# Two tiled groups per batch, with T and the slot reads in the h banks of PSUM

## The chip, the cores and the metric

The kernel runs on one core of a Trainium2 chip. The metric is the device time of one execution in microseconds (us). The engines named below are TensorE (PE, matmuls; PEld is its weight load), VectorE (DVE), ScalarE (ACT), GpSimd (POOL) and SyncE (SP, which only starts transfers here). PSUM, the memory that matmuls write to, has eight banks of 512 fp32 values per partition, as the kernel's pools divide it.

## The reference

An attention block is followed by a feed-forward block. For each of 8 batches and 8 heads there are 512 tokens `x` and 32 slots `state`, each of width 64:

```python
scores = scale * np.matmul(x, state.transpose(0, 1, 3, 2))
a = softmax(scores)                      # over the 32 slots
xread = np.matmul(a, state)              # 512 rows per head
scores2 = scale * np.matmul(state, x.transpose(0, 1, 3, 2))
a2 = softmax(scores2)                    # over the 512 tokens
sread = np.matmul(a2, x)                 # 32 rows per head: the slot reads
y = concatenate([xread, sread], axis=2)  # heads side by side: 4352 rows of 512
h = y @ w_in                             # 512 -> 2048
g = s * relu(h) ** 2 + b
out = g @ w_out                          # 2048 -> 512
```

(`softmax` stands here for the reference's max, exp and division.)

## The kernel before, in words

**The products.** The same scores serve both softmaxes. For a batch b, `T_mm` multiplies the state by the transposed tokens: T holds the scores of all 8 heads, in two PSUM banks (one per half of the tokens), 16 small matmuls of 64x32 weights with 256 columns. `E_exp` on ACT takes four exponentials of it (E, with row sums that serve the second softmax). `D_mm` sums E over the slots of each head, `D_ln` and `D_exp` make the reciprocal R of that sum, and `a4_mul` multiplies E by R: a is the first softmax, transposed. The token reads are never made. Instead `M_mm` multiplies the state by w_in (M, four chunks c of 512 columns; each chunk is 8 small matmuls into two banks), `M_cast` copies each bank into SBUF (one on DVE, one on ACT, or as the planner likes), and `h_mm` computes h = a x M, 16 blocks f of 128 columns, two matmuls each. `relu` on ACT reads a block of h, `square` on DVE squares two blocks at once. The scalars `s` and `b` are applied to the output.

The second product, o, is made for batch 0 in the plain way (`rows_mm`) and for batches 1 to 7 by a scheme of seven products of half matrices in place of eight (`STEPS`, `step_mm`), which needs sums of g blocks (`pair_sums`: pd, on DVE) and of w_out blocks (`weight_sum`: u). Two banks hold o, and DVE empties them (`step_out`), after which POOL or SP sends the rows out.

The slot reads of a batch are V (`V_mm`: E transposed by the tokens, 32 small matmuls of 64 columns). E is transposed by a DMA on SP's queue (`aT_dma`), the result is scaled by `V_copy` on DVE and transposed once more by a DMA (`sr_dma`). All eight batches' slot reads are multiplied at the very end, as h_sr and osr.

**Tiled mode.** T, M, V and one sum for the bias use parts of the TensorE array (`tp=` gives the part): several such small matmuls run beside one another. Everything else uses the whole array. The name "tiled group" is used below for tiled matmuls that follow one another with nothing else between.

**PSUM.** Eight banks: pool `psA` (planner's name "att") has four, for T of batches 2 to 7, D, M, V and small things; `psH` ("h") has two, for h; `psO` has two, for o. T of batches 0 and 1 uses the o banks, which are free then.

**The order.** Nothing is ordered by hand. Every piece of work is given to a planner by `add` with its engine and estimated duration, a priority key (lower goes first), what it needs and makes, and the buffers it uses. `Plan.order` plays the work through on its own clock, and the kernel then issues the instructions of every engine in the order found. On the chip each engine follows its order strictly and waits by semaphore where something isn't ready. The table K holds the numbers that keys are made of. For the work around the change (lines 654 to 749): T of batch b has key `kT`, the four M chunks have `kM[0..3]`, and V has `kV`, each an operation of its own; the planner adds 0.1 to the duration when the tiled mode changes, and prefers tiled work while it is in tiled mode. Lines 128 to 131 model a load: `channel` is the time when the DMA channel is free.

**The loads.** `SEQ` (line 374) is the order in which POOL starts the loads of w_in (wi0 to wi3), w_out (wo0 to wo3) and tokens of batches 0 to 3 in fp16 (x0 to x3). The fp16 tokens of batches 0 and 1 are read only by V; those of later batches are also transposed by DMA for T (`dma_xT`). Batches 0 and 1 have their tokens transposed on TensorE instead (`xT_mm`) from an fp32 load at the start. `filler` is a matmul on zeros [...].

Of the kernel before, what the change touches and what calls it, by code (L numbers as in the profile page):

```python
# [13 lines left out]
class Plan:  # L14
# [13 lines left out]
    def order(self, filler, fill_until, ready):  # L28
# [46 lines left out]
        while done_n < len(ops) and now < getattr(self, "horizon", 1e9):  # L75
            for e in free_at:
                if free_at[e] > now + 1e-9:
                    continue
                best = None
                alone = False  # L80
                if e == "PE" and not mode:
                    near = [i for i in cand[e] if ops[i][7] and since[i] <= now + 0.3 and soon(i) <= now + 0.3]
                    alone = len(near) < 2 or sum(len([b for b in ops[i][5] if self.pool_of[b] == "att"]) for i in near[:2]) > (
                        self.caps["att"] - sum(x not in freed for x in allocs["att"])
                    )
                look = self.look if e in ("ACT", "DVE") else 0.06
                for i in cand[e]:
                    if since[i] > now + look:
                        continue
                    t = soon(i) - now  # L90
                    if t > look:
                        continue
                    k = ops[i][1] + 20.0 * max(0.0, t)
                    if e == "PE" and ops[i][7] and mode:
                        k -= 4.0
                    if alone and ops[i][7]:
                        k += self.solo if now < 40.0 else self.late
                    if len(ops[i][0]) > 1 and e == "DVE":
                        k += ops[i][9]
                        if free_at["ACT"] <= now + 0.3:  # L100
                            continue
                    if best is None or k < best[0]:
                        best = (k, i, t)
                if best is not None and best[2] > 1e-9:
                    continue
                if best is None:
                    fill = 0.22
                    if e == "PE" and now < fill_until and not allocs["h"] and not any(since[i] < now + fill for i in cand[e]):
                        free_at[e] = now + fill
                        times.append(free_at[e])  # L110
                        log.append((now, len(log), "PE", filler, "warm", free_at[e]))
                    continue
                i = best[1]
                engs, key, fn, needs, makes, bufs, land, tiled, after, spare = ops[i]
                for x in engs:
                    cand[x].discard(i)
                for b in bufs:
                    if b not in placed:
                        placed.add(b)
                        allocs[self.pool_of[b]].append(b)  # L120
                dur = engs[e]
                if e == "PE":
                    dur += 0.1 * (tiled != mode)
                    mode = tiled
                end = done = now + dur
                if land is not None:
                    kind, span = land
                    if kind == "load":
                        done = max(channel, end + 2.0) + span
                        channel = max(channel, done)  # L130
                        done += 0.8
                    elif kind == "tp" and e == "SP" and now < channel + 4.0:
                        done = end + max(span, min(8.0, 6.0 - 0.75 * (now - channel)))
                        channel = max(channel, now + 2.0) + 1.1
                    else:
                        done = end + span
                free_at[e] = end
                times.append(end)
                times.append(done + self.hop)
                for m in makes:  # L140
                    ready[m], made_on[m] = done, (e if land is None else None)
                for m in makes:
                    for j in waits.pop(m, ()):
                        count[j] -= 1
                        if count[j] == 0:
                            settle(j)
                for b in bufs:
                    users[b] -= 1
                    if users[b] == 0:
                        freed[b] = done + self.hop  # L150
                done_n += 1
                log.append((now, len(log), e, fn, makes, end))
# [9 lines left out]
def kernel(  # L162
# [21 lines left out]
    P = 128  # L184
# [25 lines left out]
    def att_ps(shape, dtype, name):  # L210
        return psA.tile(shape, dtype, tag="att", name=name)
# [45 lines left out]
    for i in range(4):  # L257
# [15 lines left out]
    ident32 = konst.tile([P, P], FP32, name="ident32")  # L273

    K = dict(
        h1=18.7, hs=1.0, M0=-6.0, M1=3.8, T1=10.0, x2=31.5, T2=21.6, D2=25.6, M2=44.7, V0=39.2, V1=31.3, u=25.2,
        us=-12.3, pd1=16.9, o0=20.4, o2=33.9, w=24.1, r=5.8, T=-9.2, D=7.2, Mb=4.3, V=9.4, S=2.5, S0=-1.1,
        E=-2.4, L=-5.7, E0=-4.8, L0=10.2, E1=-17.5, L1=-2.0, a4=-9.1, Mc=13.9, pd=19.2, solo=18.7, f0=6.6,
        f1=17.4, mc=-12.6, hsr=-6.4, Ssr=-3.2, jE00=18.1, jE01=15.1, jL00=3.9, jL01=20.6, jR00=5.7, jR01=-5.2,
        jE10=5.7, jE11=-10.7, jL10=-6.2, jL11=-11.3, jR10=0.8, jR11=-2.5, jM0=-2.7, jM1=2.1, xc=3.9, a2=31.2,  # L280
        lx=10.0, la=5.4, lb=12.1, rs=33.5, xs=10.6, x1=10.8, rL=6.4, a4L=-9.7, McL=4.7, mcL=2.1, soloL=3.3,
    )
    A = {b: {"E": {}, "a4": {}} for b in range(B)}
    G, PD, U, SN, OSB = {}, {}, {}, {}, {}
# [40 lines left out]
    def PEt(t):  # L325
        return ("PE", t)
# [44 lines left out]

    gate = konst.tile([P, 2], FP16, name="gate")
    nc.gpsimd.tensor_copy(gate, xf_part(0, 2)[:, 0, 0:2])
    SEQ = "wi0 wi1 wi2 wo0 wo1 wi3 wo2 x2 wo3 x0 x1 x3"
    seq = [(t[:-1], int(t[-1])) for t in SEQ.split()]
    for n, it in enumerate(seq):
        key = -40 + n
# [107 lines left out]
    def xT_copy(b, p):  # L485
# [5 lines left out]

        return fn

    def st_T(b, g, q, m):
        h = head_of(g, q)
        if b < 4:
            return A[b // 2]["stT"][64 * m : 64 * m + 64, 8 * (b % 2) + h]
        return stTd[64 * m : 64 * m + 64, (b - 4) * NG + h // 4, 32 * (h % 4) : 32 * (h % 4) + 32]

    def T_mm(b, gs):  # L500
        def fn(e):
            a = A[b]
            if gs[0] == 0:
                if b < 2:
                    a["T"] = [ob[m].rearrange("p (g t) -> p g t", g=NG) for m in range(2)]
                else:
                    a["T"] = [att_ps([P, NG, S // 2], FP32, f"T_{b}_{m}") for m in range(2)]
            for q in range(4):
                for g in gs:
                    h = head_of(g, q)  # L510
# [100 lines left out]

    def V_mm(b):
        def fn(e):
            ps = A[b]["V"] = att_ps([P, NG, D], FP32, f"V_{b}")
            for g in range(NG):
                for c in range(SCH):
                    for q in range(4):
# [36 lines left out]
    for b in range(B):  # L654
# [5 lines left out]
            kM = [8 * c + (K["M0"] if b == 0 else K["M1"]) for c in range(4)]  # L660
        elif b == 2:
            kx, kT, kD = K["x2"], K["T2"], K["D2"]
            kM = [K["M2"] + i for i in range(4)]
        else:
            kT = NKF * b + K["T"]
            kx, kD = kT - 12, kT + K["D"]
# [9 lines left out]
        if b < NB_T:  # L676
            for p in range(4):
                ps = ("att", f"xTps{b}{p}")
                kp = kx + K["xs"] * p
                add(  # L680
                    PEt(0.55), kp, xT_mm(b, p), [("xf", b, p), "ident32"] + ([("xTps", b, p - 1)] if p else []),
                    [("xTps", b, p)], [ps, ("u", f"xf{2 * b + p // 2}"), xT_b],
                )
                add(
# [8 lines left out]
                )  # L693
        xT_need = [("xTh", b, p // 2, p % 2) for p in range(4)] if b < NB_T else [("xT4", b, i) for i in range(4)]
        E_b = [("E0", f"E{b}0"), ("E1", f"E{b}1"), ("rs", f"rs{b}")]
        Tb = [("att", f"T{b}0"), ("att", f"T{b}1")] if b >= 2 else []
        if b == 0:
            for g in range(2):
                add(
                    PEt(0.2), kT, T_mm(b, [g]), [("stT", b), ("xTh", b, g, 0), ("xTh", b, g, 1)] + ([("T", b, 0)] if g else []),  # L700
                    [("T", b, g)], Tb + [xT_b] + stT_b + E_b, tiled=True,
                )
        else:
            add(
                PEt(0.22), kT, T_mm(b, [0, 1]), [("stT", b)] + xT_need + ([("E", 0, 0), ("E", 0, 1)] if b == 1 else []),
                [("T", b, 0), ("T", b, 1)], Tb + [xT_b] + stT_b + E_b, tiled=True,
            )
        for g in range(2):
            Eb, Rb, a4b = (f"E{g}", f"E{b}{g}"), (f"R{g}", f"R{b}{g}"), (f"a4{g}", f"a4{b}{g}")
# [16 lines left out]
                add(AC(0.63), K["rs"] + 2 * b + g, E_sum(b, g), [("E", b, g)], [("sum", b, g)], [Eb, rs], after=24.0)  # L726
        q_need = [("sum", b, 0), ("sum", b, 1)] if b < 2 else [("E", b, 0), ("E", b, 1)]
        add(DV(0.25), kD + 4, q_rec(b), q_need, [("q", b)], [rs, ("q", f"q{b}")])
        M_b = ("M", f"M{b}")
        for c in range(4):  # L730
            mp = [("att", f"M{b}{c}{g}") for g in range(2)]
            add(
                PEt(0.22), kM[c], M_mm(b, c), [("stT", b), ("wi", c)], [("Mps", b, c)], mp + stT_b + [M_b],
                tiled=True,
            )
            for g in range(2):
                kc = kM[c] + K["Mc" if b < 2 else "McL"] + K.get(f"jM{b}", 0.0)
                add(
                    (AC(0.53), DV(0.6)) if g else (DV(0.6), AC(0.53)), kc, M_cast(b, c, g),
                    [("Mps", b, c)], [("M", b, c, g)], [mp[g], M_b], spare=K["mc" if b < 2 else "mcL"],  # L740
                )
        kV = [K["V0"], K["V1"]][b] if b < 2 else NKF * b + K["V"]
        V_b = ("att", f"V{b}")
        add(
            PEt(0.22), kV, V_mm(b), [("aT", b, 0), ("aT", b, 1)] + ([("x", b, i) for i in range(4)] if b < 2 else []), [("V", b)],
            [V_b, ("aT", f"aT{b}"), xn_b], tiled=True,
        )
        add(DV(0.25), kV, V_copy(b), [("V", b), ("q", b)], [("sr", b)], [V_b, ("sr", f"sr{b}"), ("q", f"q{b}")])
        add(("SP", 1.2), kV, sr_dma(b), [("sr", b)], [("srT", b)], [("sr", f"sr{b}")], ("tp", 4.0))


# [401 lines left out]
```

The softmax here doesn't subtract the row's maximum and nothing guards it: scores larger than these inputs give would overflow.

## Time and profile before

| what | value |
|---|---|
| median of 4 runs | 210.35 us (209.77 to 211.1) |
| the profiled execution: its own time | 209.84 us |
| the profiled execution: span of the trace | 208.0 us |
| DVE g squares (L791), 64 | 43.5 us, 685 ns each |
| ACT ReLU of h (L784), 127 | 73.4 us, 600 ns each |
| M casts on ACT (L305), 37 | 20.6 us, 602 ns each |
| M casts on DVE (L307), 27 | 17.8 us, 685 ns each |
| matmuls of Mps, 256 | started from 12.7 to 151.4 us |
| matmuls of T in att banks, 96 | started from 51.3 to 147.8 us |
| matmuls of V, 256 | started from 43.8 to 172.9 us |

The page gives busy time of each engine and, in the slices, its share in each of 40 equal parts of the span. A row of a group has the line, the engine, what is written from what, the count, and the mean duration. The duration of a matmul includes its passage through the array, so matmuls that follow one another overlap in the rows; how long one occupies TensorE is read from the distance between starts.

### The profile page before, as it was taken

How to read it: one execution, taken by the hardware profiler on the slowest of the kernel's cores; microseconds unless marked ns; L12 is line 12 of the kernel's file. 1: busy time of each engine (PE TensorE's matmuls, PEld its weight loads, DVE VectorE, ACT ScalarE, POOL GpSimd, SP SyncE). 2: the span in 40 equal slices, each digit the busy share in tenths (PEclk: the TensorE clock that was granted, in tenths of full speed). 3: DMA queues.
4: the chain of work that ended last, by engine and by line, in shares of the span. 5: the costliest groups of instructions: out<-in, count | busy, mean ns of one | idle time of the engine just before them, and what ended most of it. 6: DMA issues, size and time to landing. Idle time of an engine off the chain costs nothing.

```text
span 208.0 us, 4904 instructions
## 1 busy us (share of the span) xinstructions
PE 202.6 (97%) x1957; PEld 133.2 (64%) x1957; DVE 168.1 (81%) x334; ACT 133.1 (64%) x297; POOL 42.8 (21%) x67
## 2 busy tenths in 40 slices
PE   7998999999999999999999999999999999999993
PEld 3743444343866775577667775777657777888882
DVE  3589988988768997989999997898789969686552
ACT  2579999875688468985398548954886545354000
POOL 0861000241160244011521134021102110110000
PEclk9999999999999999999999999999999999999999
DMA  6999999999999346961496338721212110311033
GB/s 193 306 204 195 205 209 190 175 245 144 187 168 159 110 126 126 138 102 50 103 138 126 106 76 140 146 101 52 81 31 101 48 58 6 104 40 62 4 125 126
DMA packets 44423, 26.05 MB, mean 125 GB/s; under 512 B 26480, under 2 KB 42608, under 8 KB 44400
## 3 DMA queue, kind: packets, MB, share of 16 engines
q0 software_dynamic: 14976, 15.73, 41.3%
q1 hardware_dynamic: 29136, 9.84, 24.5%
q8 instruction: 15, 0.25, 0.5%
q10 hardware_dynamic: 288, 0.16, 0.3%
q14 instruction: 8, 0.07, 0.1%
HBM read 19.43 MB, written 8.91 MB: 136 GB/s over the span
## 4 chain that ended last, share of the span: by engine, by line
PE 77%; DMA 16%; POOL 3%; DVE 1%; SPq 0%; issue 0%
PE o L214 44%; PE h L214 20%; DMA wo<-in_moe_w_out_dram 10%; DMA aT<-E 4%; PE h_sr L214 3%; PE osr L214 3%; PE Mps L214 3%; DMA xf<-in_x_dram 2%; POOL wi L342 1%; PE D L214 1%; PE V L214 1%; POOL wo L352 1%; PE T L214 1%; SPq L256 0%; POOL xn L365 0%; DVE c_sr L1040 0%
## 5 line engine op out<-in xcount | busy, mean ns | idle before, releaser
L784 ACT ACTIVATE g<-h 128x512 f16<-128x512 f32 x127 | 73.4, 600 | 28.4 <-PE h L214 27.1
L214 PE MATMUL h<-a,M 128*128 128x512 f16 x256 | 73.4, 379 | 0.6 <-ACT g L784 0.5
L214 PEld LDWEIGHTS <-pd 128*128 128x128 f16 x448 | 42.8, 98 | 19.9 <-issue 2.2
L214 PEld LDWEIGHTS <-g 128*128 128x128 f16 x400 | 38.7, 98 | 18.5 <-issue 1.4
L214 PE MATMUL o<-u,pd 128*128 128x256 f16 x336 | 49.8, 273 | 0.0
L791 DVE TENSOR_TENSOR g<-g 128x1024 f16<-128x1024 f16 x64 | 43.5, 685 | 4.7 <-ACT g L784 4.1
L214 PE MATMUL o<-wo,g 128*128 128x256 f16 (+1 forms) x288 | 45.3, 296 | 0.0
L1052 POOL DMA_DIRECT2D out_dram<-c x24 | 16.4, 682 | 105.1 <-DVE c L1040 96.9
L214 PEld LDWEIGHTS <-M 128*128 128x128 f16 x256 | 24.4, 98 | 12.8 <-issue 3.8
L1040 DVE SCALAR_TENSOR_TENSOR c<-o,sb_cols,bias_bc 128x512 f32<-128x512 f32 x28 | 21.0, 750 | 9.4 <-PE o L214 8.8
L305 ACT CAST M<-Mps 128x512 f16<-128x512 f32 x37 | 20.6, 602 | 8.1 <-PE Mps L214 8.0
L1040 DVE SCALAR_TENSOR_TENSOR c<-o,sb_cols,c 128x512 f32<-128x512 f32 x21 | 15.7, 749 | 6.8 <-PE o L214 6.6
L807 DVE TENSOR_TENSOR pd<-g 128x1024 f16<-128x1024 f16 x28 | 19.1, 683 | 0.1
L307 DVE CAST M<-Mps 128x512 f16<-128x512 f32 x27 | 17.8, 685 | 0.4
L214 PE MATMUL o<-u,g 128*128 128x256 f16 x112 | 16.6, 273 | 0.0
L365 POOL DMA_DIRECT2D xn<-in_x_dram x20 | 15.8, 828 | 3.9 <-DMA wi<-in_moe_w_in_dram 3.4
L214 PE MATMUL o<-wo,pd 128*128 128x256 f16 x112 | 15.1, 273 | 0.0
L816 DVE TENSOR_TENSOR pd<-g,pd 128x512 f16<-128x512 f16 x28 | 12.0, 430 | 0.3
L818 DVE TENSOR_TENSOR pd<-g,pd 128x512 f16<-128x512 f16 x28 | 11.8, 422 | 0.5
L529 ACT ACTIVATE E<-T 128x256 f16<-128x256 f32 x24 | 8.9, 384 | 5.1 <-PE T L214 5.0
L560 ACT ACTIVATE R<-L 128x512 f16<-128x512 f32 x16 | 10.1, 630 | 0.5
L553 ACT ACTIVATE L<-D 128x512 f32<-128x512 f32 x16 | 9.4, 595 | 1.2 <-PE D L214 1.0
(81 smaller groups left out, 160.6 us busy)
## 6 DMA issues: line engine op xcount, KB each, us to landing
out_dram<-c POOLq DMA_DIRECT2D x24, 256.0 KB, 2.5
xf<-in_x_dram SPq DMA_DIRECT2D x8, 256.0 KB, 4.8
wi<-in_moe_w_in_dram POOLq DMA_DIRECT2D x4, 512.0 KB, 8.5
wo<-in_moe_w_out_dram POOLq DMA_DIRECT2D x4, 512.0 KB, 16.1
xn<-in_x_dram POOLq DMA_DIRECT2D x4, 512.0 KB, 21.8
xn<-in_x_dram POOLq DMA_DIRECT2D x16, 128.0 KB, 4.4
out_dram<-osb POOLq DMA_DIRECT2D x4, 256.0 KB, 4.2
out_dram<-c SPq DMA_DIRECT2D x4, 256.0 KB, 2.5
```

Source lines behind the costliest of these rows:

```text
L214: return nc.tensor.matmul(out, lhsT, rhs, start=start, stop=stop, tile_position=tp, is_transpose=is_transpose, skip_group_check=True,)
L305: nc.scalar.copy(dst, src)
L307: ENG[e].tensor_copy(dst, src)
L365: nc.gpsimd.dma_start(out=xn[b][:, h0:h1].rearrange("p h c d -> p h (c d)"), in_=x[b, h0:h1].rearrange("h (q c) d -> q h (c d)", q=P),)
L560: nc.scalar.activation(A[b][f"R{g}"], A[b][f"L{g}"], AF.Exp, scale=-1.0)
L784: nc.scalar.activation(g_of(name, f), OSB["h", name, f], AF.Relu)
L791: ENG[e].tensor_mul(g, g, g)
L807: nc.vector.tensor_tensor(pd[:, :, 0:2], g4[:, :, 1:2, :].to_broadcast((P, 2, 2, t)), g4[:, :, 0:4:3, :], ALU.subtract,)
L816: nc.vector.tensor_tensor(pd[:, :, 2], g4[:, :, 3], pd[:, :, 0], ALU.subtract)
L818: nc.vector.tensor_tensor(pd[:, :, 3], g4[:, :, 2], pd[:, :, 2], ALU.subtract)
L1040: nc.vector.scalar_tensor_tensor(t, src, s_bc, add, ALU.mult, ALU.add)
L1052: ENG[e].dma_start(dst[:, rows:SCH:2, hD * h : hD * h + hD], SN[b, name])
```

## The change

In batches 2 to 7, T and the M chunks 0 and 1 are made one operation for the planner, with T's key, and the M chunks 2 and 3 and the slot reads of another batch a second one, with the key of chunk 2: batch 2 takes V of batch 0, batch 3 takes V of batches 1 and 2, and batches 4 to 7 take V of the batch before. V of batch 7 remains alone. For batches 0 and 1, T and the M chunks stay as they were. T of batches 2 to 7 and every V are written to banks of psH in place of psA. A helper `several` runs functions one after the other.

With it the planner's numbers change: nearly the whole table K, the modelled landing of a load before 15 us (0.1 behind the channel in place of 0.8), the duration of `xT_mm` (0.45 in place of 0.55), and x1 is loaded before x0.

```diff
-                        done += 0.8
+                        done += 0.8 if done > 15.0 else 0.1
...
-        h1=18.7, hs=1.0, M0=-6.0, M1=3.8, T1=10.0, x2=31.5, T2=21.6, D2=25.6, M2=44.7, V0=39.2, V1=31.3, u=25.2,
...
+        h1=16.1, hs=1.0, M0=-6.0, M1=4.5, T1=13.8, x2=17.3, T2=21.6, D2=23.7, M2=46.3, V0=38.1, V1=37.9, u=27.3,
...
-    SEQ = "wi0 wi1 wi2 wo0 wo1 wi3 wo2 x2 wo3 x0 x1 x3"
+    SEQ = "wi0 wi1 wi2 wo0 wo1 wi3 wo2 x2 wo3 x1 x0 x3"
...
+    def several(*fs):
+        def fn(e):
+            for f in fs:
+                f(e)
+
+        return fn
...
-                    a["T"] = [att_ps([P, NG, S // 2], FP32, f"T_{b}_{m}") for m in range(2)]
+                    a["T"] = [psH.tile([P, NG, S // 2], FP32, tag="h", name=f"T_{b}_{m}") for m in range(2)]
...
-            ps = A[b]["V"] = att_ps([P, NG, D], FP32, f"V_{b}")
+            ps = A[b]["V"] = psH.tile([P, NG, D], FP32, tag="h", name=f"V_{b}")
...
-            kM = [K["M2"] + i for i in range(4)]
+            kM = [K["M2"], K["M2"], K["M2"] + K["Mb"], K["M2"] + K["Mb"]]
...
-                    PEt(0.55), kp, xT_mm(b, p), [("xf", b, p), "ident32"] + ([("xTps", b, p - 1)] if p else []),
+                    PEt(0.45), kp, xT_mm(b, p), [("xf", b, p), "ident32"] + ([("xTps", b, p - 1)] if p else []),
...
-        Tb = [("att", f"T{b}0"), ("att", f"T{b}1")] if b >= 2 else []
+        Tb = [("h", f"T{b}0"), ("h", f"T{b}1")] if b >= 2 else []
...
+        if b >= 2:
+            vs = {2: [0], 3: [1, 2]}.get(b, [b - 1])
+            add(
+                PEt(0.66), kT, several(T_mm(b, [0, 1]), M_mm(b, 0), M_mm(b, 1)),
+                [("stT", b), ("wi", 0), ("wi", 1)] + xT_need,
+                [("T", b, 0), ("T", b, 1), ("Mps", b, 0), ("Mps", b, 1)],
+                Tb + [xT_b] + stT_b + E_b + mps[0] + mps[1] + [M_b], tiled=True,
+            )
+            add(
+                PEt(0.44 + 0.2 * len(vs)), kM[2], several(M_mm(b, 2), M_mm(b, 3), *[V_mm(v) for v in vs]),
+                [("stT", b), ("wi", 2), ("wi", 3)] + sum([V_needs[v] for v in vs], []),
+                [("Mps", b, 2), ("Mps", b, 3)] + [("V", v) for v in vs],
+                stT_b + mps[2] + mps[3] + [M_b] + sum([V_bufs[v] for v in vs], []), tiled=True,
+            )
...
-        kV = [K["V0"], K["V1"]][b] if b < 2 else NKF * b + K["V"]
...
+        kV = NKF * b + K["V"]
+        if b == B - 1:
+            add(PEt(0.22), kV, V_mm(b), V_needs[b], [("V", b)], V_bufs[b], tiled=True)
```

`V_needs` and `V_bufs` are lists of what V of each batch needs and uses, as before but with an h bank. The casts of M, the copies of V and their transfers stay operations of their own.

More of the change, by code (lines that the diff above doesn't have):

```diff
@@ L275 @@
     K = dict(
-        h1=18.7, hs=1.0, M0=-6.0, M1=3.8, T1=10.0, x2=31.5, T2=21.6, D2=25.6, M2=44.7, V0=39.2, V1=31.3, u=25.2,
[L277 to L281, printed above, removed]
+        h1=16.1, hs=1.0, M0=-6.0, M1=4.5, T1=13.8, x2=17.3, T2=21.6, D2=23.7, M2=46.3, V0=38.1, V1=37.9, u=27.3,
+        us=-13.3, pd1=13.7, o0=25.7, o2=34.4, w=23.8, r=4.7, T=-9.2, D=10.2, Mb=5.5, V=-3.3, S=3.3, S0=-1.1,
+        E=-3.5, L=-5.8, E0=-4.8, L0=0.4, E1=-10.7, L1=-2.6, a4=-9.1, Mc=10.1, pd=19.7, solo=18.2, f0=6.0,
+        f1=17.4, mc=-12.4, hsr=-8.2, Ssr=2.8, jE00=17.6, jE01=14.7, jL00=5.7, jL01=21.9, jR00=5.9, jR01=-2.7,
+        jE10=2.7, jE11=-4.4, jL10=-8.1, jL11=-22.4, jR10=-2.0, jR11=-2.5, jM0=-1.9, jM1=6.2, xc=1.5, a2=38.2,
+        lx=9.7, la=8.1, lb=11.1, rs=29.4, xs=-1.4, x1=10.8, rL=1.3, a4L=-14.8, McL=5.6, mcL=1.9, soloL=8.6,
     )
@@ L702 @@
                 )
-        else:
+        elif b == 1:
             add(
-                PEt(0.22), kT, T_mm(b, [0, 1]), [("stT", b)] + xT_need + ([("E", 0, 0), ("E", 0, 1)] if b == 1 else []),
+                PEt(0.22), kT, T_mm(b, [0, 1]), [("stT", b)] + xT_need + [("E", 0, 0), ("E", 0, 1)],
                 [("T", b, 0), ("T", b, 1)], Tb + [xT_b] + stT_b + E_b, tiled=True,
+            )
+        M_b = ("M", f"M{b}")
+        mps = [[("att", f"M{b}{c}{g}") for g in range(2)] for c in range(4)]
+        V_needs = [[("aT", v, 0), ("aT", v, 1)] + ([("x", v, i) for i in range(4)] if v < 2 else []) for v in range(B)]
+        V_bufs = [[("h", f"V{v}"), ("aT", f"aT{v}"), ("xn", f"x{v}")] for v in range(B)]
+        if b >= 2:
[11 more added lines that the diff above has]
+                stT_b + mps[2] + mps[3] + [M_b] + sum([V_bufs[v] for v in vs], []), tiled=True,
             )
@@ L728 @@
         add(DV(0.25), kD + 4, q_rec(b), q_need, [("q", b)], [rs, ("q", f"q{b}")])
-        M_b = ("M", f"M{b}")
         for c in range(4):
[L731 to L735, printed above, removed]
+            mp = mps[c]
+            if b < 2:
+                add(
+                    PEt(0.22), kM[c], M_mm(b, c), [("stT", b), ("wi", c)], [("Mps", b, c)], mp + stT_b + [M_b],
+                    tiled=True,
+                )
             for g in range(2):
@@ L741 @@
                 )
-        kV = [K["V0"], K["V1"]][b] if b < 2 else NKF * b + K["V"]
[L743 to L748, printed above, removed]
+        kV = NKF * b + K["V"]
+        if b == B - 1:
+            add(PEt(0.22), kV, V_mm(b), V_needs[b], [("V", b)], V_bufs[b], tiled=True)
+        add(DV(0.25), kV, V_copy(b), [("V", b), ("q", b)], [("sr", b)], [V_bufs[b][0], ("sr", f"sr{b}"), ("q", f"q{b}")])
         add(("SP", 1.2), kV, sr_dma(b), [("sr", b)], [("srT", b)], [("sr", f"sr{b}")], ("tp", 4.0))
```

## The prediction

> **What bounds the kernel now.** I read the page first, then the list of waits, then the order of time on TensorE. The page's busy row and slices:
>
> ```profile
> PE 202.6 (97%) x1957; PEld 133.2 (64%) x1957; DVE 168.1 (81%) x334; ACT 133.1 (64%) x297; POOL 42.8 (21%) x67
> PE   7998999999999999999999999999999999999993
> PEclk9999999999999999999999999999999999999999
> ```
>
> TensorE is busy in every slice but the first and the last, at full clock. Busy alone is no proof, because matmuls overlap. The list of waits, asked for TensorE alone, has only these two:
>
> ```profile
> PE warm_ps L214 <- DVE warm L229: 1.2, 1, 1.2
> PE h L214 <- ACT g L784: 0.5, 1, 0.5
> ```
>
> The second is at 17.86 us. After that TensorE never waits visibly for anybody until its last matmul at 204.3, so the time is the sum of what TensorE streams plus the gaps between streams. From distances of starts, one h matmul (128x512) takes 0.216 us and one o matmul (128x256) 0.109. Counting each group so, gaps of about 6.2 us remain after 20 us, nearly all of them beside matmuls in tiled mode (T, Mps, V). The order of time around 103 us shows how they are read (start, duration, then what):
>
> ```profile
> 101.73 0.41 PE L214 MATMUL Mps<-wi,stTd 64*32 64x512 f16 x8
> 102.07 0.42 PE L214 MATMUL V<-xn,aT 128*32 128x64 f16 x32
> 102.42 0.39 PE L214 MATMUL o<-u,pd 128*128 128x256 f16 x2
> 102.65 0.59 PE L214 MATMUL h<-a,M 128*128 128x512 f16 x2
> 103.17 0.43 PE L214 MATMUL T<-xT,stTd 64*32 64x256 f16 x16
> 103.40 0.42 PE L214 MATMUL Mps<-wi,stTd 64*32 64x512 f16 x8
> 103.75 0.61 PE L214 MATMUL o<-u,pd 128*128 128x256 f16 x4
> 104.20 0.59 PE L214 MATMUL h<-a,M 128*128 128x512 f16 x2
> 104.63 1.47 PE L214 MATMUL o<-u,pd 128*128 128x256 f16 x12
> 105.94 1.03 PE L214 MATMUL h<-a,M 128*128 128x512 f16 x4
> ...
> 107.33 0.63 PE L214 MATMUL Mps<-wi,stTd 64*32 64x512 f16 x16
> 107.89 0.60 PE L214 MATMUL h<-a,M 128*128 128x512 f16 x2
> ```
>
> The o run at 102.42 has 2 matmuls: 0.23 to the next start, its own stream. The h pair at 102.65 streams until 103.08 (2 x 0.216), but T starts at 103.17: 0.09 to enter tiled mode. T takes 0.23, one M product 0.22, and the next o starts at 103.75: 0.13 to leave. **A tiled group thus costs 0.22 us besides its work.** Two M products in one group (107.24, where the o stream ends, to 107.89) take 0.65 = 2 x 0.216 + 0.22. One M and a V (101.64 to 102.42) take 0.78; V alone (172.61 to 173.05, the same way) takes 0.44. So V's work is 0.22, and going from M to V inside a group costs 0.78 - 0.22 - 0.22 - 0.22 = 0.12.
>
> **The change, part by part.** (1) **Fewer tiled groups.** For batches 2 to 7, and V of batches 0 and 1 which moves into them, the old order has 21 tiled groups, starting at 39.01, 41.83, 43.79, 47.34, 48.86, 51.04, 67.39, 70.67, 81.67, 85.61, 87.57, 101.73, 103.17, 107.33, 123.43, 125.74, 129.47, 145.14, 147.66, 151.17 and 172.70. The new order has two for each of six batches, and V of batch 7: 13. Eight groups less by 0.22 is -1.76 us. A step from M to V stands in three old groups (101.73, 123.43, 145.14) and in six new ones: +3 x 0.12 = +0.36. T beside M costs no such step (0.67 = 0.23 + 0.22 + 0.22).
>
> (2) **V of batches 0 and 1.** Their old group at 43.79 takes 0.94 from stream to stream, of which 2 x 0.22 + 0.22 = 0.66 is explained. The other 0.28 is the wait for the last transposed E, issued at 35.95 and landed at 44.36 in the chain of waits. Both V now come later, with M products of batches 2 and 3: -0.28. What hides it is that transpose being long done; if V of batch 0 came as early as now, 0.28 stays. On SP's queue their slot-read transposes come later too; their reader is h_sr at 179 us. POOL's loads of x4 to x7 take buffers that x0 and x1 free later, but the first two have free ones, and the others start no earlier than 100 us by the plan.
>
> (3) **T in both h banks.** While T holds them no h matmul can start. The trace gives the length of the hold, since E on ACT reads T:
>
> ```profile
> 103.70 0.38 ACT L529 ACTIVATE E<-T 128x256 f16<-128x256 f32 x1 [0.91 <-PE T L214]
> ...
> 104.79 0.39 ACT L529 ACTIVATE E<-T 128x256 f16<-128x256 f32 x1
> 105.05 0.22 ACT L529 ACTIVATION_READ_ACCUMULATOR E<-T 128x1 f32 x1
> 105.14 1.10 ACT L784 ACTIVATE g<-h 128x512 f16<-128x512 f32 x2
> ```
>
> From T's start (103.17) to the fourth E's end is 2.1 us. The new group itself fills 0.66 of it to the exit (0.23 + 2 x 0.216) and the switch out, so about 1.3 us must be filled by o, which is 12 o matmuls. Just these 12 ran at 104.63 in the old order; one h pair alone stood in the window. Before T, both h banks must also be read, which is one ReLU (0.60) after the last h, another 6 o matmuls. Runs of 20 o (2.18 us) stand in the chain of waits at 91.13, 112.84, 121.32 and 134.54 with no gap. *Here a rule speaks against the change:* the Trainium skill, Perfetto Trace Analysis, Optimizing Tensor Performance, wants independent matmul groups to rotate through different PSUM banks, so that one's evacuation overlaps the next one's matmuls; T in both h banks ends that rotation for h. If TensorE stood for it, 1.3 us by 6 batches is +7.8 us, a slower kernel. By the row, o has two banks of its own and covers it: 0. I take the row, and +0.2 in all for a batch in which o is one short. Queued behind the waiting group on TensorE's own order are h and o, all of them, so a cover that fails is lost in full.
>
> (4) **V in an h bank, four M banks at once.** V holds its bank from 102.07 until its copy at 102.84 has ended (0.28), 1.05 us, while h keeps the other. A batch of h is 16 x 0.43 = 6.9 us of a 22.0 us cycle (T starts at 81.67 and 147.66, three cycles apart), so h has room: 0. The group of T needs all four attention banks free. D shares them, but in the old order D comes at 111.16, 5.9 us after E, so waiting for a cast (0.60 on ACT, 0.69 on DVE) is hidden. T also waits for the M buffer now, that is for h of two batches before; the old order already has M of the same batch within 1.5 us of T (101.73 and 103.17). VectorE is the near bound: 20.1 of 22 us in the windows 81 to 103 and 103 to 125. It gets no instruction more, but batch 3's eight casts move from about 48 to behind 70, where the window 57 to 81 has 19.3 of 24 us: room for four of 0.69.
>
> (5) **The first 20 us.** The plan counts loads before 15 us as landed 0.7 earlier. wi0 was issued at 6.11 and took 5.9, landing at 12.0, while M starts at 12.70 behind filler matmuls. So there is 0.7 us at most, if all that follows moves along; it need not, because wo0 comes only at 20.7 and ACT is 6.7 of 8 us busy. A new order of the first 40 us could also lose as much. Both ends: -0.7 and +0.7. I take -0.35, as the fillers at 10.88 and 13.82 are time that nothing needs. The swap of x0 and x1 in POOL's load order serves V alone: 0. Smaller planned transposes cost what they cost.
>
> **Sum:** -1.76 + 0.36 - 0.28 + 0.2 - 0.35 = -1.83 us. The profiled execution took 209.84 (span 208.0), so 208.0; the median of the runs shown, 210.35, lies 0.51 above it, giving **208.5 us**. What is late next is still TensorE.
>
> **Rivals.** *A, the cover fails (slower).* Place: behind each T group, batches 2 to 7. It needs six banks at once, and h must have paused for a ReLU beforehand and four E afterwards. If the o matmuls are not ready there (their sums come from a VectorE that is 91% busy, and a bank drain of 0.75 stands at each step's end), TensorE stands. It decides from (1.68 + 0.35) / 6 = 0.34 us per batch. At 0.75 each, half the uncovered 1.3 plus a late drain, it is +4.5 - 2.0 = +2.5: 212.9. For it: DVE's load. Against: the o runs above, and that TensorE had no wait of this kind at all.
>
> *B, given back once (no change).* M of batch 2 was cast between 39.7 and 44.9, long before T at 51.26; now its casts start with T, on the engine of E, L and R. Two casts of 0.60 delay a4 and the first h of batch 2 (57.11) by 1.2 us. If the o left over from batches 0 and 1 does not stretch, that idle comes once and the head gains nothing: -1.83 + 0.35 + 1.2 = -0.3, or 210.1. For it: no h at all runs from 46.4 to 57.1. Against: T can come earlier, since batch 0's h are done by then.
>
> *C, the change does not do what it says:* groups remain split by the hardware's own waits inside them. A group has one place in the order and nothing can come between, so I give it no time of its own.
>
> **How the numbers follow.** My forecast 0.60 (own range 207.4 to 209.3: full head gain and no shortfall gives -2.4, plus the scatter of the runs), B 0.18, A 0.22. About 0.5% or 1.05 us is what a measurement here can tell from no change. Faster: the forecast nearly whole and a bit of B, 0.60. Same: 0.17. Slower: 0.23. The range goes from 207.4 to 211.8, leaving out the worse half of A.
>
> **What would show it.** Right: 13 tiled groups after the h of batch 0, each of the first kind about 0.88 us from stream to stream (0.23 + 0.43 + 0.22), each of the second 1.00 (0.43 + 0.22 + 0.12 + 0.22); no rows in TensorE's waits behind E or casts; M starting at 12.0 to 12.3. Wrong: waits of TensorE on ACT's E, or gaps of over 0.3 us within 3 us of each T; VectorE above 95% between 57 and 81; a first h of batch 2 later than 57.

## The result, and the profile after

The changed kernel takes 209.57 us (median of 44 runs), the kernel before 210.43 (63 runs): a ratio of **0.9958, interval 0.9946 to 0.9970**. The time fell by about 0.9 us where 1.83 was forecast; 209.57 lies inside the range, 1.1 us above the 208.5. The profiled execution took 209.46, with a span of 207.7. Medians here are of all runs; ratios leave out the few runs that were slow as a whole, so a ratio need not be the quotient of two medians.

TensorE is still the engine that everything hangs on. Its list of waits has become longer (what waited, for whom, us in total, times, longest):

```profile
...
PE h L214 <- ACT g L806: 0.7, 3, 0.3
PE Mps L214 <- ACT E L536: 0.5, 1, 0.5
PE o L214 <- DVE osb L966: 0.3, 1, 0.3
PE xTps L214 <- DMA xf<-in_x_dram: 0.3, 1, 0.3
PE D L214 <- DVE M L307: 0.2, 1, 0.2
```

Most of the new rows are from the first 20 us. Those of o behind VectorE's osb and of D belong together, and are the subject of what follows. First the part that went as planned, in TensorE's order of time around the groups of batch 4 (start, duration):

```profile
93.11 0.43 PE L214 MATMUL T<-xT,stTd 64*32 64x256 f16 x16
93.33 0.64 PE L214 MATMUL Mps<-wi,stTd 64*32 64x512 f16 x16
93.90 1.48 PE L214 MATMUL o<-wo,g 128*128 128x256 f16 x12
95.22 0.38 PE L214 MATMUL D<-E,bones 128*128 128x512 f16 x1
...
97.93 0.63 PE L214 MATMUL Mps<-wi,stTd 64*32 64x512 f16 x16
98.49 0.42 PE L214 MATMUL V<-xn,aT 128*32 128x64 f16 x32
98.84 0.39 PE L214 MATMUL o<-u,pd 128*128 128x256 f16 x2
```

The first group takes 0.89 us from the end of the stream before it to the next start, the second 1.00, as the prediction worked out (0.88 and 1.00). And h pauses without a cost: 12 o matmuls and the D follow at 93.90 with nothing between (12 x 0.109 = 1.31, and 95.22 - 93.90 = 1.32). Batches 3 to 7 all look so.

Batch 2 does not. The same view, 46 us earlier:

```profile
47.24 0.43 PE L214 MATMUL T<-xT,stT 64*32 64x256 f16 x16
47.47 0.64 PE L214 MATMUL Mps<-wi,stT 64*32 64x512 f16 x16
48.04 1.04 PE L214 MATMUL o<-wo,g 128*128 128x512 f16 x4
49.41 0.38 PE L214 MATMUL o<-wo,g 128*128 128x256 f16 x2 [0.33 <-DVE osb L966]
50.01 0.39 PE L214 MATMUL D<-E,bones 128*128 128x512 f16 x1 [0.23 <-DVE M L307]
```

Four o matmuls of 512 columns stream 0.86 us, so the next one could have started at 48.90; it starts at 49.41, waiting for its bank to be read. Two of 256 columns take 0.22, so D could have come at 49.63; it starts at 50.01, waiting for a cast to free an attention bank. **Together 0.89 us in which TensorE streams nothing**, once in the kernel.

To compare whole executions I count gaps as the prediction did: distance of starts less the stream of what started, over all matmuls (fillers count as gaps). After 22 us, the kernel before has 6.46 us of gaps and the changed one 5.65, so 0.81 less, nearly the whole difference of the medians. Of the 5.65, the 4.5 us that begin with T of batch 2 hold 1.05, where about 0.2 belongs to the tiled group.

Why is the bank read late? VectorE's order of time, changed kernel:

```profile
43.54 1.70 DVE L813 TENSOR_TENSOR g<-g 128x1024 f16<-128x1024 f16 x2
45.16 1.09 DVE L829 TENSOR_TENSOR pd<-g 128x1024 f16<-128x1024 f16 x1
...
48.61 0.74 DVE L966 SCALAR_TENSOR_TENSOR osb<-o,sb_cols,bias_bc 128x512 f32<-128x512 f32 x1
49.27 0.68 DVE L307 CAST M<-Mps 128x512 f16<-128x512 f32 x1
```

Elsewhere two squares take 1.28 and such a sum 0.68; here 1.70 and 1.09, so 0.83 us more. VectorE works without a pause up to 48.61, when it comes to the o bank; the cast for D stands behind that. What ran beside it from 43.99, in POOL's order of time:

```profile
43.99 1.72 POOL L307 CAST st<-stf 128x512 f16<-128x512 f32 x2 [2.23 <-DMA stf<-in_state_dram]
```

These are the casts of the state of batches 4 to 7 (line 417 of the kernel before). The kernel before has them at the same time (43.43 to 45.04), but there T of batch 2 comes only at 51.26. The Trainium skill, SBUF — State Buffer, Terms, says that VectorE and GpSimd arbitrate for one pair of ports to SBUF, the memory that both work on. Two theories stand against each other: VectorE was late because POOL slowed it (*shared port*), or D waited because a joined group holds all four attention banks (*bank hold*).

### The profile page after: what moved, and what is told of

The parts are those of the page before. It is cut to its first block, busy times and chain, and to the rows that moved or that the text cites. A ratio compares the mean times of both kernels' runs of the same rounds, so it can differ in the third digit from the quotient of the medians.

```text
span 207.7 us, 4900 instructions
## 1 busy us (share of the span) xinstructions
PE 200.6 (97%) x1956; PEld 132.6 (64%) x1956; DVE 172.1 (83%) x340; ACT 131.2 (63%) x291; POOL 43.2 (21%) x67
## 4 chain that ended last, share of the span: by engine, by line
PE 87%; DVE 6%; ACT 3%; DMA 2%; issue 0%; SPq 0%
PE o L214 45%; PE h L214 25%; PE Mps L214 3%; PE h_sr L214 3%; PE osr L214 3%; DMA xf<-in_x_dram 2%; PE D L214 2%; PE xTps L214 2%; DVE g L813 1%; PE V L214 1%; DVE pd L829 1%; ACT g L806 1%; DVE osb L966 1%; PE T L214 1%; PE warm_ps L214 1%; DVE pd L838 1%
## 5 line engine op out<-in xcount | busy, mean ns | idle before, releaser
L214 PE MATMUL h<-a,M 128*128 128x512 f16 x256 | 71.8, 379 | 0.8 <-ACT g L806 0.7
L214 PE MATMUL o<-wo,g 128*128 128x256 f16 (+1 forms) x288 | 47.5, 296 | 0.3 <-DVE osb L966 0.3
L214 PE MATMUL o<-u,pd 128*128 128x256 f16 x336 | 46.8, 273 | 0.0
L307 DVE CAST M<-Mps 128x512 f16<-128x512 f32 x33 | 21.7, 681 | 1.2 <-PE Mps L214 1.2
L305 ACT CAST M<-Mps 128x512 f16<-128x512 f32 x31 | 17.6, 595 | 3.5 <-PE Mps L214 3.5
L829 DVE TENSOR_TENSOR pd<-g 128x1024 f16<-128x1024 f16 x28 | 19.6, 700 | 0.2
L214 PE MATMUL o<-u,g 128*128 128x256 f16 x112 | 17.8, 273 | 0.0
L214 PE MATMUL o<-wo,pd 128*128 128x256 f16 x112 | 16.5, 273 | 0.0
```

What stands on the lines that cost most here:

```text
L214: return nc.tensor.matmul(out, lhsT, rhs, start=start, stop=stop, tile_position=tp, is_transpose=is_transpose, skip_group_check=True,)
L305: nc.scalar.copy(dst, src)
L307: ENG[e].tensor_copy(dst, src)
L829: nc.vector.tensor_tensor(pd[:, :, 0:2], g4[:, :, 1:2, :].to_broadcast((P, 2, 2, t)), g4[:, :, 0:4:3, :], ALU.subtract,)
```

## The experiments

All ratios are to the kernel before, with their 95% intervals; kernels of one set ran on one chip. The changed kernel, run again beside the first set, took 209.44 us, ratio 0.9963 (0.9946 to 0.9981).

> The changed kernel once more, on the chip of the runs beside it. Ratio to before 0.996. If the late first chunk (13.06 us) was chance, this profile may show it between 12.0 and 13.0; if it comes from the change, it is again at 13.0 or later. The stop of about 0.7 us behind T of batch 2 (48.9 to 50.0) comes again in any case.

Its stop behind T of batch 2 is there again: the 4.5 us hold 1.05 us of gaps as before. The first chunk lands at 13.2 and M starts at 13.70. By the test above, that would blame the change; but the load was also issued later, at 6.99 in place of 6.06, and experiment 6 finds the same in the kernel before.

**1. The casts go to ACT.** The planner's entry and the order stay; only the engine that executes the casts changes.

```diff
-    add(("POOL", 1.7), -19, lambda e: cast_st(e, st16_2, OSB["stf2"]), ...
+    add(("POOL", 1.7), -19, lambda e: cast_st("ACT", st16_2, OSB["stf2"]), ...
```

> The two POOL casts of the state of batches 4 to 7 (about 44.0 to 45.7 us) go to ACT, which is idle there for 5 us; nothing else in the order changes. Theory 'shared port': POOL's casts hold up VectorE's squares and sums by 0.8 us, VectorE then frees the o bank and casts M late, and TensorE stops behind T of batch 2: with POOL out of the way VectorE's two operations at 43.5 and 45.2 take 0.69 each, the stop shrinks by 0.5 to 0.8 us, and the ratio to before goes from 0.996 to 0.992 to 0.993. Rival 'bank hold': the stop comes from the four attention banks that the joined group holds, so D waits as before and the time stays within 0.2 us of the changed kernel.

Measured: 208.69 us, 0.9935 (0.9906 to 0.9964), 0.75 us less than the changed kernel beside it (the intervals of the two overlap; experiment 7 repeats it). VectorE's order of time in this run:

```profile
43.50 1.28 DVE L813 TENSOR_TENSOR g<-g 128x1024 f16<-128x1024 f16 x2
44.70 0.68 DVE L829 TENSOR_TENSOR pd<-g 128x1024 f16<-128x1024 f16 x1
...
47.74 0.74 DVE L966 SCALAR_TENSOR_TENSOR osb<-o,sb_cols,bias_bc 128x512 f32<-128x512 f32 x1
48.40 0.68 DVE L307 CAST M<-Mps 128x512 f16<-128x512 f32 x1
```

The squares and the sum have their usual times, the bank is read 0.87 us earlier, and TensorE's order of time shows what it was worth:

```profile
48.00 1.26 PE L214 MATMUL o<-wo,g 128*128 128x512 f16 x6
49.14 0.39 PE L214 MATMUL D<-E,bones 128*128 128x512 f16 x1
```

Two more o matmuls run on at once and D starts at 49.14 in place of 50.01: the gaps in the 4.5 us fall from 1.05 to 0.21, the tiled group alone. The joined group and its four banks are the same as before, so the bank hold alone stops nothing.

**2. The casts twice on POOL**, the opposite dose:

```diff
-    add(..., lambda e: cast_st(e, st16_2, OSB["stf2"]), ...
+    add(..., lambda e: (cast_st(e, st16_2, OSB["stf2"]), cast_st(e, st16_2, OSB["stf2"])), ...
```

> The changed kernel with POOL's casts of the state made twice (four casts instead of two, the same values), everything else kept. Theory 'shared port': two more casts take VectorE about 0.8 us more between 45.7 and 47.5, the o bank and the M cast come later by that, and TensorE stops 0.6 to 0.9 us longer behind T of batch 2; ratio to before 0.999 to 1.001. Rival 'bank hold': within 0.2 us of the changed kernel, 0.995 to 0.997.

Measured: 210.11 us, 0.9992 (0.9972 to 1.0013); the gain of the change is used up. The wait in TensorE's list, then rows of VectorE and of POOL, put together in order of time:

```profile
PE o L214 <- DVE osb L966: 0.9, 1, 0.9
```
```profile
45.32 1.07 POOL L307 CAST st<-stf 128x512 f16<-128x512 f32 x1
45.95 0.71 DVE L838 TENSOR_TENSOR pd<-g,pd 128x512 f16<-128x512 f16 x1
46.34 0.80 POOL L307 CAST st<-stf 128x512 f16<-128x512 f32 x1
46.70 0.71 DVE L840 TENSOR_TENSOR pd<-g,pd 128x512 f16<-128x512 f16 x1
47.09 0.80 POOL L307 CAST st<-stf 128x512 f16<-128x512 f32 x1
47.34 1.09 DVE L829 TENSOR_TENSOR pd<-g 128x1024 f16<-128x1024 f16 x1
```

Each VectorE operation that starts during a cast is longer (0.71 for 0.42, 1.09 for 0.68), the bank is read at 49.26, and the gaps in the 4.5 us are 1.62: 0.57 more than in the changed kernel, a little under what was expected. VectorE's four operations beside the casts lose 1.40 us (one of 1.10 stands before these rows), the two in the changed kernel 0.83: again 0.57. Moved away and doubled, the casts move the stop both ways.

The rows show how, too. The casts end at 46.38, 47.13 and 47.88, the VectorE operations at 46.66, 47.41 and 48.43. The second and third cast here end 0.47 us after the VectorE operation that began before them, and the VectorE operations end 0.28, 0.28 and 0.55 us after the cast that began before them. So the two engines take turns, and a row holds a wait and then the work. Shared port is shown: something that only one of the two can have at a time. That it is a pair of ports is the skill's word; the trace shows the turns.

**3. The casts on ACT in the kernel before** (the same one-word edit).

> The same edit in the kernel before: its two POOL casts of the state go to ACT, the order is kept. Theory 'VectorE had room there before': VectorE's sum at 43.86 gets its 0.42 back in place of 0.72, but no matmul waited for it, so the ratio to before is 0.999 to 1.001. Rival 'the casts cost in every order': 0.996 or less, as in the changed kernel.

Measured: 211.13 us, 1.0037 (1.0014 to 1.0061). Slower, which neither theory had. TensorE's waits name a new one:

```profile
PE T L214 <- DMA xT<-xn: 1.3, 1, 1.3
```

T of batch 2 waits for its transposed tokens. POOL, no longer busy with the casts, had gone on to its next work, the 512 KB load of x3, at 44.17 in place of 45.12, while SP's four transposes of x2 (issued 40.42 to 45.95) were under way; the longest transpose of tokens landed 8.3 us after its issue, where the longest in two profiles of the kernel before took 6.0 and 6.4. To test this, one more gate holds that load:

```diff
                 nc.gpsimd.tensor_copy(gate, A[1]["aT"][:, :, 0, 0])
+                nc.gpsimd.tensor_copy(gate, A[1]["sr"][:, 0:2])
```

> The kernel before with its casts on ACT, as in before_st_act, and POOL's load of x3 held until the slot reads of batch 1 are scaled (about 45.3 us), which is where it started in the kernel before; without that POOL, relieved of the casts, started it at 44.2. Theory 'the earlier load collided with the transposes of x2, and T of batch 2 waited 1.3 us for them': the wait goes, ratio to before 0.998 to 1.001. Rival 'the casts on ACT themselves cost': again 1.003 or more.

Measured: 210.51 us, 1.0001 (0.9978 to 1.0024), and the wait is gone (the load started at 46.53, later than meant; the longest transpose took 6.7). So the casts cost nothing that can be measured in the kernel before, on POOL or on ACT; moving them only let a load start beside transposes that T needed. How the load delays them, no run shows. In the changed kernel the x3 load comes at 51.56, and with the casts on ACT at 50.78, behind T, and so escapes this.

**4. The price of a tiled group.** In each of the twelve joined groups the next matmuls of the order are put between T and M, and between M and V:

```diff
+        if isinstance(step[3], list):
+            step[3][0](step[2])
+            held.append(step[3][1])
+            continue
         step[3](step[2])
+        if step[2] == "PE" and held:
+            held.pop()(step[2])
```

> In each of the twelve joined groups the next matmuls of the order (an o or an h block) are put between T and M, and between M and V, so that 12 tiled groups are added and everything else stays. Theory 'a tiled group costs 0.22 us': six T|M cuts at 0.22 and six M|V cuts at 0.22 less 0.12 are +1.9 us against the changed kernel, ratio to before 1.005. Rival 'the gaps are covered elsewhere': less than +0.6 us.

Measured: 211.89 us, 1.0092 (1.0064 to 1.0120), 2.45 us above the changed kernel. The gaps after 22 us rise by 2.53 us. Batch 3 shows a cut between T and M:

```profile
75.69 0.43 PE L214 MATMUL T<-xT,stT 64*32 64x256 f16 x16
76.06 0.39 PE L214 MATMUL o<-u,pd 128*128 128x256 f16 x2
76.38 0.63 PE L214 MATMUL Mps<-wi,stT 64*32 64x512 f16 x16
```

From the end of the stream before T (75.60) to the next start behind M (76.94) are 1.34 us, of which the two o take 0.22; the joined group takes 0.89. So this cut costs 0.23. Between M and V it is 0.09 (0.65 and 0.44 apart, 1.00 together). Five and six of them are 1.7, the cut at batch 2 lying inside the stop. Three gaps of 0.20 come with the new neighbours, between one o and the next; about 0.2 us stay unexplained. A tiled group costs what was claimed, and pulling the groups apart costs some gaps besides.

**5. The joined groups with all old numbers**: the new code, but the old table K, load model, transposes and order of x0 and x1.

> The joined groups and the h banks alone, with all of the old numbers (table K, landing of a load, transposes, order of x0 and x1). Theory 'the count of tiled groups is the gain, and the new numbers only keep the waits away': the gaps at tiled groups fall by 1.6 us as in the changed kernel, and new waits on TensorE take 1 to 2 us of it back; ratio to before 0.996 to 1.002. Rival 'the numbers are the gain': no better than 1.005.

Measured: 209.29 us, 0.9959 (0.9937 to 0.9980), no different from the changed kernel. The gaps after 22 us are 5.60, against 6.46 before. Here T of batch 2 comes at 50.81, the casts stay on POOL (43.45), and there is no stop (about 0.2 in the 4.5 us); but before 77.30 there is one of 0.65 for an o bank that VectorE reads late, behind three casts of M, with no cast on POOL. So the grouping brings the gain, and in either numbering about half of it is lost at one late VectorE read. The many new numbers bring nothing that can be measured.

**6. The first 20 us.** A second profile of the kernel before:

> The kernel before once more, for a second profile. What is asked is when the first w_in chunk lands and TensorE starts M (12.0 and 12.70 us in the first profile). Theory 'the head is chance': the landing moves by about 1 us from one execution to another with the same program. Rival 'the new order made it late': the landing is again within 0.2 us of 12.0.

M starts at 13.44, not 12.70, with the same program: POOL's gate opened at 7.13 in place of 5.98. Over all profiles with an unedited head M starts between 12.66 and 13.83, and two executions of one program differ by 0.74 and 0.58, so a single pair of profiles can't be compared there. What can be: the gaps before 22 us against the start of M. With M at 12.70 the kernel before has 9.55 us, with M at 12.66 the new order (in the run with split groups) has 9.81; at 13.44 and 13.12 it is 10.27 and 10.02. For the same start of M the new order thus has 0.1 to 0.3 us more. Five profiles with the old head have 9.55 to 10.42 (mean 9.92), six with the new one 9.81 to 10.79 (mean 10.10). No gain is seen.

Two edits of the best version press on it. One adds two fillers (0.43 us) ahead of the first M, where they also cut a tiled group:

> The changed kernel with the casts on ACT, and two more filler matmuls (0.43 us) between T of batch 1 and the first M; the tiled group there is cut, so 0.65 us in all if nothing covers it. Theory 'the landing sets M': M waited 0.5 us for the chunk in two of four profiles, so 0.1 to 0.3 us on the median. Rival 'the planned order sets M': the full 0.65 us.

Measured: 209.32 us, 0.9946 (0.9925 to 0.9968). The median is 0.63 above 208.69, as if the planned order counted in full; but the two ran on different chips, and by the ratios (0.9946 against 0.9935, intervals overlapping) it is 0.23 us, as 'the landing sets M' has it. This run's profile shows a wait of 0.9 us for the chunk (M at 14.88). It stays open which of the two counts. The other opens POOL's gate earlier (`xf_part(0, 1)` for `xf_part(0, 2)`):

> The changed kernel with the casts on ACT, and POOL's gate before the first w_in load opened by the second part of x instead of the third, some 0.7 us earlier; the order is kept. Theory 'the head hangs on the landing of the first w_in chunk': M starts 0.4 to 0.7 us earlier and most of it reaches the end, ratio to before 0.990 to 0.991. Rival 'the DMA engines are full anyway': the chunk lands as late as before, or x lands later by as much, and the ratio stays at 0.9935.

Measured: 208.73 us, 0.9917 (0.9887 to 0.9946). The interval holds both expectations. In the profile the chunk was issued at 5.16 and took 7.3 us, and M started at 13.08, no earlier. It stays open whether an earlier gate helps.

**7. The best version again**, the changed kernel with the casts on ACT:

> The changed kernel with the casts on ACT once more, for a narrower interval as the best version so far: ratio to before 0.991 to 0.994, some 0.8 us less than the changed kernel.

Measured: 208.63 us, 0.9898 (0.9860 to 0.9937), from six runs; a little below what was expected. With the first measurement (0.9935) it lies 0.65% to 1.0% below the kernel before, and the interval lies below the changed kernel's (0.9946 to 0.9970).

## Why the prediction fell short, point by point

- **TensorE is the bound; gaps at tiled groups are the thing to save.** Right. 13 tiled groups remain from 47 us on. The gaps before were 6.46 us after 22 us by the full count, a little more than the "about 6.2" after 20.
- **Steps 1 and 2: -1.76 + 0.36 - 0.28 = -1.68.** Right, in mechanism and size. With the stop taken away (experiment 1), the gaps after 22 us are 4.80, against 6.46: -1.66. Group by group, the 21 old groups hold 5.32 us besides their work and the 13 new ones 3.73, which is -1.59; the wait of 0.28 at 43.79 is in it.
- **Step 3, T in both h banks: "+0.2 in all for a batch in which o is one short".** This is the term that failed most. With step 4's wait for a cast, which was put at nothing, it measured 0.84 us, all at batch 2. The mechanism of the step holds: o covers the pause in batches 3 to 7, so the rule of rotating banks cost nothing there. But the cover of the pause is itself served by VectorE, which must free o's bank. I looked at how many o matmuls stood ready, not at whether the engine behind them was on time at that one place, where T moved up from 51.26 to 47.24. By the rows this wait is 0.51 us.
- **Step 4, casts and banks.** That D's waiting for a cast is hidden was wrong at batch 2, by the other 0.38 us, and the wait there was VectorE's lateness too. The reason given was a D that came 5.9 us after E in the old order; in the new one D comes 1.9 to 2.8 us after T starts. The window 57 to 81 was no trouble: VectorE was busy for 20.2 of 24 us. What mattered were the 5 us before T of batch 2, in which it was busy for 4.86.
- **Step 5, the first 20 us: -0.35.** It measured about zero: the gaps after 22 us account for 0.81 of the 0.86. M does not start earlier. In some profiles it waits for the chunk (0.55 us in experiment 1), in others it follows T of batch 1, which now stands before it, without a wait (12.43, then 12.66, with split groups). h then waits for ACT 0.7 in place of 0.5.
- **The sum.** -1.68 + 0.84 and nothing from the head gives -0.84; the medians moved by -0.86. The waits behind T (0.64 more than the 0.2) and the head (0.35) are the whole miss.
- **The rivals.** B had the right shape, a loss given back once at batch 2, with the wrong cause: not two casts in front of a4 (the first h of batch 2 came at 55.61, not later than 57.11), but an o bank read late. A named the right engine, yet it happened once and not in six batches.

## What to carry to other kernels

When a bottleneck engine is filled by independent work during a pause, follow that work to the engine that frees its buffers, and look at that engine's backlog in the few microseconds before the pause; a busy share over 20 us doesn't show it. A single late instruction cost half of what eight removed groups had brought. And moving work off a side engine also moves whatever that engine does next: here a load, which then ran into transfers that TensorE needed.

## What the runs showed of the hardware

- A VectorE operation with two fp16 inputs in SBUF that starts during one of POOL's casts takes 0.71 us in place of 0.42 (128x512) or 1.09 in place of 0.68 (128x1024), and casts that start during such an operation end 0.47 us after it (0.80 to 1.07 us a row in experiment 2). The Trainium skill's page SBUF — State Buffer (Terms) tells of an exclusive lock, held for the whole instruction, in which the loser blocks fully; the rows of experiment 2 agree, with the two engines taking turns. Two casts cost VectorE 0.83 us and not their own 1.72, because nearly half of that is their own wait (an estimate: 2 x 0.47 of it is work).
- A load of 512 KB that started 0.95 us earlier came with a token transpose that landed after 8.3 us, against a longest of 6.0 to 6.7 in the profiles without it, and with a wait of 1.3 us on TensorE; with the load held back the wait was gone.
- The first w_in chunk, issued between 5.2 and 7.3 us after the start, took 5.8 to 8.6 us to land, for the same transfer; the start of M scatters by about 1 us (12.66 to 13.83).
